# Packed attention and a gated feed-forward block on one core: the first entry's query softmax in four pieces of tokens, another form of the weight conversion, and a new order of all steps

## The chip, the cores and the metric

The program runs on one core of one Trainium2 chip. The metric is device microseconds of one execution, the median of several runs; lower is better. Five engines work beside each other, each on its own list of instructions: TensorE (PE in the profile), VectorE (DVE), ScalarE (ACT), GpSimd (POOL) and SyncE (SP), which issues nearly all transfers.

## The reference

```python
def _attn_ref(q, k, v, p):             # q, k, v: (8, 8, 576, 64); p: (8, 8, 32, 64)
    def sm_attn(qq, kk, vv):           # softmax over the last axis, scale 1/8
        ...
    p_packed = sm_attn(p, k, v)        # 32 packed rows read 576 tokens
    return sm_attn(q, p_packed, p_packed)

def _moe_ref(x, w_in, w_spatial, b_spatial, w_out):   # x: (8, 576, 512)
    h = np.maximum(x @ w_in, 0.0)                     # 512 -> 1024
    u, v = h[..., :512], h[..., 512:]
    v_n = (v - mean(v)) / sqrt(var(v) + 1e-6)         # over features
    v_s = einsum('ts,bsd->btd', w_spatial, v_n) + b_spatial
    return (u * v_s) @ w_out                          # 512 -> 512
```

`w_in` and `w_out` arrive as float64 and are turned into float32 on the chip. All the rest is float32.

## The kernel before, in words

The batch has eight entries. Each goes through the same stages, all on chip: packed scores, maximum, exponential and sum (`pack_*`), the packed rows (`packed*`), the query scores and their softmax over 32 packed rows (`query_*`), the feed-forward values (`value`, `relu`, `moments`, `mean`, `inverse`, `norm*`), the spatial gate (`gate*`) and the output product (`product`, `put`). The output of the query softmax is never multiplied out: `mix` multiplies the packed rows by `w_in`, so that `value` and `up` are products of the softmax weights `a` with those mixed weights `m`. Every float32 factor of a large product is split into a rounded high part and the rest (`*_hi` on ScalarE, `*_lo` on VectorE or GpSimd, by `rest`), and three products hi·hi, hi·lo, lo·hi are made. From entry 1 on, the gate and the output product are done with seven block products in place of eight; entry 0 does the gate plainly (`gate`, all of `hm`, `l` and `t` terms) because its spatial weights are still being prepared (`spatial_hi`, `spatial_rest`, `spatial_lo`; `spatial_rest(c)` is the identity pass `x - high(x)` on TensorE, four passes of 288 columns in float32 and two rounded ones).

There are four PSUM tiles of two banks, `ps0` to `ps3`; every product takes one with `on(i)` and must wait until its last reader, often a copy on ScalarE, is done. SBUF tiles have tags with one or two buffers; the mixed weights `m_h`, `m_l` have one buffer each, the query weights `a_h`, `a_l` too.

The order of work is written out by hand: `InOrder` with `PIN = "tvsg"` pins TensorE, VectorE, ScalarE and GpSimd to the order of the calls in the program's text. An instruction that waits holds up all that stand behind it on its engine. In the text below a call such as `F6.norm_lo(2)` is a step of the feed-forward of entry 6, `A7.mix(0)` one of the attention of entry 7; while entry b runs, the attention of entries b+1, b+2 and b+3 is being prepared.

Steps that the prediction speaks of: `to_f32`, the conversion of a float64 weight (a generator; each `next` issues its next part); `pack_max` and `pack_exp` (maximum and exponential of the packed scores); `pack_turned_part` (copies of the turned weights from PSUM into `p1T`); `query_spread`, `query_max`, `query_sub`, `query_exp`, `query_add`, `query_total`, `query_inverse`, `query_norm`, `query_turn`, `query_hi`, `query_lo` (the softmax over 32 rows, in this order, on tile `sm_t`, then `extra`, then `a_h`, `a_l`); `mix_hi`, `mix_lo`, `mix_keep` (PSUM to `m_h`, `m_l`, or to `kept` first); `packed_turned` (PSUM to `ppT`); `gate_add`, `gate_mult`, `block_lo` (tiles `o`, `u`, `g_l`). Nearly all instructions are recorded at line 43 of the kernel, the wrapper, so the rows go by tiles.

Of the kernel before, what the change touches and what calls it, by code (L numbers as in the profile page):

```python
# [49 lines left out]
def body(ctx: ExitStack, tc, q, k, v, vt, p, w_in, w_sp, b_sp, w_out, out):  # L50
# [311 lines left out]
    class Attention:  # L362
# [28 lines left out]
        def pack_most(self, r):  # L391
# [40 lines left out]
        def pack_turn(self, t1, t2):  # L432

            p1 = self.p1
            self.t1, self.t2 = t1(), t2
            for r in range(2):
                for c in range(NC):
                    x = r * TAIL + c * P  # L440
                    flip(self.t1[:, r, c * P : (c + 1) * P], p1[:, r, x : x + P])
            flip(self.t2[:, 1, :P], p1.rearrange("p r s -> p (r s)")[:, NC * P : NC * P + P])
# [16 lines left out]

        def pack_values(self, psum):  # L460
            v_sb = loaded.pop(("v", self.b))
            self.pv = psum()
# [1779 lines left out]
```

## Time and profile before

| | |
|---|---|
| median of 3 runs | 392.48 us (392.11 to 392.54) |
| span of the profiled execution | 391.2 us |
| median of the runs less that span | 1.3 us, what lies around it |
| busy share of the span: PE, DVE, ACT, POOL | 96%, 83%, 72%, 39% |
| the chain that ended last, shares | PE 77%, DVE 10%, ACT 6%, POOL 3%, DMA 2%, issue 1% |
| first large product (`value` of entry 0) | 27.41 us from the span's start |
| end of the last product | 387.16 us |

A busy PE here is the time from the start of a product to its modelled end, which for a 288-column product is some 0.3 us, while the next one starts some 0.13 us after it; so the share of 96% hides waits of up to 0.2 us before each product, and the starts of products tell more than the share. The profiled execution is not one of the three timed ones; its span is taken as the base of the sum and 1.3 us is put on top.

### The profile page before, as it was taken

The numbers are of one execution on the slowest core, as the hardware profiler recorded it, in microseconds if no ns is written. First come the engines' busy times: TensorE is split into PE (matmuls) and PEld (weight loads), VectorE is DVE, ScalarE is ACT, GpSimd is POOL, SyncE is SP. The second block draws the span as 40 slices with busy tenths as digits, with TensorE's granted clock in tenths as the row PEclk, the third lists the DMA queues.
The fourth block names the chain that finished last, engine by engine and source line by source line (L and its number), as shares of the span: only waits on it lengthen the run. The fifth ranks groups of instructions, "written<-read, shape, count | busy, mean of one in ns | idle before, by whom it ended". The sixth has DMA issues, their size and how long they took to land.

```text
span 391.2 us, 8947 instructions
## 1 busy us (share of the span) xinstructions
PE 376.8 (96%) x3674; PEld 337.8 (86%) x3674; DVE 326.5 (83%) x502; ACT 280.3 (72%) x494; POOL 153.5 (39%) x190
## 2 busy tenths in 40 slices
PE   6889999999999999999999999999899999999995
PEld 5668978799798898998899898998699889999995
DVE  2898989995799959997799959997599969997784
ACT  3588876978975598766985598666895589558642
POOL 3467647899461040702143040703153043504120
PEclk9899999999999999999999999999999999999999
DMA  7999149630510803045300803033000600002003
GB/s 302 416 391 368 68 137 361 252 111 12 185 69 0 335 29 131 0 164 201 116 10 0 331 34 124 0 122 121 4 1 2 241 3 2 0 34 89 2 0 122
DMA packets 17660, 47.79 MB, mean 122 GB/s; under 512 B 1362, under 2 KB 11602, under 8 KB 14804
## 3 DMA queue, kind: packets, MB, share of 16 engines
q1 hardware_dynamic: 17332, 47.02, 32.3%
q8 instruction: 29, 0.48, 0.5%
q10 hardware_dynamic: 288, 0.21, 0.2%
q14 instruction: 11, 0.09, 0.1%
HBM read 37.79 MB, written 9.44 MB: 121 GB/s over the span
## 4 chain that ended last, share of the span: by engine, by line
PE 77%; DVE 10%; ACT 6%; POOL 3%; DMA 2%; issue 1%; SPq 0%; DVEq 0%; ACTq 0%
PE ps_t L43 77%; DMA kT<-in_k 2%; DVE u L43 2%; DVE o L43 1%; ACT vr L43 1%; DVE bn L43 1%; POOL bits L43 1%; DVE vr L43 1%; DVE sm_t L43 1%; POOL sm_t L43 1%; POOL rstd L43 1%; DVE v_l L43 1%; DVE m_l L43 1%; DVE sm L43 1%; ACT sm_t L43 0%
## 5 line engine op out<-in xcount | busy, mean ns | idle before, releaser
L43 POOL TENSOR_TENSOR u<-o,u 128x576 f32<-128x576 f32 x14 | 24.1, 1722 | 71.1 <-DVE o L43 70.6
L43 PE MATMUL ps_t<-t,wout_h 128*128 128x288 f32 x232 | 50.2, 300 | 0.1
L43 POOL TENSOR_TENSOR rstd<-mv,eps 128x2 f32<-128x2 f32 (+2 forms) x26 | 5.8, 222 | 107.2 <-DVE mv L43 107.2
L43 PE MATMUL ps_t<-wb_h,v_h 128*128 128x288 f32 x144 | 40.7, 300 | 0.5 <-ACT kept L43 0.3
L43 PEld LDWEIGHTS ps_t<-t,wout_h 128*128 128x128 f32 x232 | 37.8, 188 | 3.0 <-DVE t L43 2.4
L43 PE MATMUL ps_t<-wb_l,v_h 128*128 128x288 f32 x144 | 39.9, 295 | 0.0
L43 PE MATMUL ps_t<-a_h,m_h 128*128 128x288 f32 x128 | 38.6, 301 | 1.1 <-ACT ppT L43 1.1
L43 DVE TENSOR_TENSOR v_l<-vr,v_h 128x512 fp32r<-128x512 f32 x45 | 31.7, 727 | 7.9 <-ACT v_h L43 7.9
L43 PE MATMUL ps_t<-a_l,m_h 128*128 128x288 f32 x128 | 37.8, 295 | 0.0
L43 PE MATMUL ps_t<-a_h,m_l 128*128 128x288 f32 x128 | 37.8, 295 | 0.0
L43 PE MATMUL ps_t<-t,wout_l 128*128 128x288 f32 x116 | 32.4, 295 | 0.0
L43 PEld LDWEIGHTS ps_t<-wb_h,v_h 128*128 128x128 f32 x144 | 27.0, 188 | 5.1 <-issue 1.4
L43 PE MATMUL ps_t<-g_h,wout_h 128*128 128x288 f32 x104 | 29.2, 296 | 0.9 <-ACT pp L43 0.9
L43 PE MATMUL ps_t<-wsums,v_h 128*128 128x288 f32 x168 | 29.3, 296 | 0.0
L43 PE MATMUL ps_t<-g_h,wout_l 128*128 128x288 f32 x104 | 29.1, 295 | 0.0
L43 ACT CAST v_h<-vr 128x512 fp32r<-128x512 f32 x46 | 27.3, 624 | 2.3 <-DVE vr L43 1.6
L43 PE MATMUL ps_t<-wb_h,v_l 128*128 128x288 f32 x144 | 28.5, 294 | 0.0
L43 PEld LDWEIGHTS ps_t<-wb_l,v_h 128*128 128x128 f32 x144 | 27.1, 188 | 0.0
L43 PE MATMUL ps_t<-m_h,a_h 128*128 128x512 f32 x80 | 26.0, 392 | 0.1
L43 PEld LDWEIGHTS ps_t<-a_h,m_h 128*128 128x128 f32 x128 | 24.0, 188 | 2.3 <-ACT ppT L43 1.3
L43 DVE BATCH_NORM_STATS2 bn<-vr 128x6 f32<-128x512 f32 x32 | 21.1, 681 | 5.7 <-ACT vr L43 5.7
L43 PE MATMUL ps_t<-m_l,a_h 128*128 128x512 f32 x80 | 25.9, 390 | 0.0
(178 smaller groups left out, 1188.4 us busy)
## 6 DMA issues: line engine op xcount, KB each, us to landing
v_sb<-in_v SPq DMA_DIRECT2D x8, 1024.0 KB, 6.6
kT<-in_k SPq DMA_DIRECT2D x7, 1152.0 KB, 5.1
qT<-in_q SPq DMA_DIRECT2D x7, 1152.0 KB, 5.1
out_t<-prod SPq DMA_DIRECT2D x27, 288.0 KB, 2.4
raw<-in_w_in SPq DMA_DIRECT2D x4, 1024.0 KB, 9.4
raw<-in_w_out SPq DMA_DIRECT2D x2, 1024.0 KB, 7.9
kT<-in_k SPq DMA_DIRECT2D x2, 576.0 KB, 7.1
qT<-in_q SPq DMA_DIRECT2D x2, 576.0 KB, 12.4
```

What stands on the lines that cost most here:

```text
L43: return lambda *a, **k: self.tc.keep_in_program_order(call(*a, **k))
```

## The change

What it does, in five parts:

1. `to_f32`: the test for tiny numbers stands first (`max` of the magnitude with a least value, in place) and the last pass that multiplied by the outcome of a comparison is gone; GpSimd's sum writes the result. For the two halves of `w_in` that are needed first, the magnitude is taken on VectorE and no longer on ScalarE.
2. `pack_max` of entry 0 takes the maximum by halves of the keys, the first while the second half is still to come; scale and the smaller of both (negated) maxima are one instruction. The turned weights are copied row by row, one row on VectorE.
3. The query softmax of entry 0 runs in four pieces of tokens (128, 160, 96 and 192 of 576) in place of two halves.
4. `spatial_rest` makes its identity passes two and two.
5. All steps from the first to the last entry stand in a new order; the PSUM tile that a product takes changes with it. Two warming products of 2 (`keep_warm`) are left out.

```diff
-        dve.tensor_scalar(
-            bits, high, 3, 0x3FFFFFFF, op0=ALU.logical_shift_left, op1=ALU.bitwise_and
-        )
...
+        if eng is act:
+            act.activation(size, high.bitcast(F32), AF.Abs)
+        else:
+            eng.tensor_scalar(bits, high, 0x7FFFFFFF, None, op0=ALU.bitwise_and)
+        yield
+        dve.tensor_scalar_max(size, size, LEAST)
+        yield
+        dve.tensor_scalar(
+            bits, bits, 3, 0x3FFFFFFF, op0=ALU.logical_shift_left, op1=ALU.bitwise_and
+        )
+        yield
         dve.scalar_tensor_tensor(
             bits, high, -0x40000000, bits, op0=ALU.bitwise_and, op1=ALU.bitwise_or
         )
         yield
         for j in range(raw.shape[1]):
-            pool.tensor_tensor(bits[:, j], bits[:, j], low[:, j], op=ALU.add)
-        yield
-        size = high.bitcast(F32)
-        act.activation(size, size, AF.Abs)
-        yield
-        dve.scalar_tensor_tensor(
-            dst, size, LEAST, bits.bitcast(F32), op0=ALU.is_ge, op1=ALU.mult
-        )
+            pool.tensor_tensor(dst[:, j].bitcast(I32), bits[:, j], low[:, j], op=ALU.add)
...
         for h in range(2):
-            hs = slice(h * HS, (h + 1) * HS)
-            mm(ps[:, h, :HS], ident, x[:, hs], True, False)
+            mm(ps[:, h, :HS], ident, x[:, h * HS : (h + 1) * HS], True, False)
+        for h in range(2):
             mm(ps[:, h, :HS], minus, rows_of(wb_h, wt_h, c)[:, h], False, True)
...
+            self.spans = [(0, 0, HS), (1, 0, HS)]
+            if self.by_half:
+                self.spans = [(0, 0, 128), (0, 128, HS), (1, 0, 96), (1, 96, HS)]
...
+        def pack_max_half(self, r, x):
+            if x == 0 and r == 0:
+                self.first = small.tile([P, 2], F32, tag="first", name="first")
+            to = (self.nmax if x else self.first)[:, r : r + 1]
+            dve.tensor_reduce(to, self.s1[r][:, x, :HS], axis=AX.X, op=ALU.max, negate=True)
+
+        def pack_scale_both(self, r):
+            nmax = self.nmax[:, r : r + 1]
+            dve.tensor_scalar(
+                nmax, nmax, self.first[:, r : r + 1], SCALE, op0=ALU.min, op1=ALU.mult
+            )
...
+        def pack_turned_row(self, r, eng=act):
...
+            copy(
+                self.p1T[:, :NC, r, :],
+                self.t1[:, r, :].rearrange("p (c x) -> p c x", c=NC),
+            )
```

Every `query_*` step now takes the number of a piece and works on that part of the tiles, as this one does:

```diff
-        def query_exp(self, i):
-            act.activation(self.t[i], self.t[i], AF.Exp, scale=SCALE)
+        def query_exp(self, k):
+            i, lo, hi, n = self.cut(k)
+            t = self.t[i][:, n, :]
+            act.activation(t, t, AF.Exp, scale=SCALE)
```

The order, at three places. First VectorE in entry 0, from the query scores on (`sm_t` is the softmax tile, `mx` and `sm` its maxima and sums, `extra` the turned weights). Before:

```order
L43 STREAM_TRANSPOSE sm_t<-ps_t 128x576
L43 TENSOR_REDUCE mx<-sm_t 128x18
L43 STREAM_TRANSPOSE sm_t<-ps_t 128x576
L43 TENSOR_REDUCE mx<-sm_t 128x18
L43 TENSOR_REDUCE sm<-sm_t 128x18
L43 TENSOR_SCALAR sm<-sm 128x18
L43 RECIPROCAL sm<-sm 128x18
L43 TENSOR_REDUCE sm<-sm_t 128x18
L43 TENSOR_SCALAR sm<-sm 128x18
L43 RECIPROCAL sm<-sm 128x18
L43 STREAM_TRANSPOSE extra<-sm_t 128x576
L43 TENSOR_TENSOR m_l<-ps_t,m_h 128x1024
```

And with the change, the same stretch from its second half on:

```order
L43 TENSOR_TENSOR sm_t<-sm_t,sm 128x256
L43 RECIPROCAL sm<-sm 128x10
L43 TENSOR_REDUCE mx<-sm_t 128x12
L43 STREAM_TRANSPOSE extra<-sm_t 128x256
L43 TENSOR_REDUCE sm<-sm_t 128x6
L43 STREAM_TRANSPOSE extra<-sm_t 128x320
L43 TENSOR_SCALAR sm<-sm 128x6
L43 TENSOR_TENSOR m_l<-ps_t,m_h 128x1024
L43 RECIPROCAL sm<-sm 128x6
L43 TENSOR_REDUCE sm<-sm_t 128x12
L43 TENSOR_SCALAR sm<-sm 128x12
L43 RECIPROCAL sm<-sm 128x12
```

The first turned piece (256 columns, 128 tokens) now comes out while the last two pieces are still being summed, and `m_l`, the rest of the mixed weights, stands behind the second turned piece.

Second, ScalarE at the end of entry 0, ahead of its first output product (`t`, `g_h` and `wout_h` are high parts of that product's factors, `m_h` that of entry 1's mixed weights, `pp` the packed rows of entry 2, whose PSUM tile the product takes). Before:

```order
L43 CAST t<-u 128x576
L43 CAST m_h<-ps_t 128x1024
L43 CAST g_h<-u 128x576
L43 CAST a_898<-bits 128x512
L43 ACTIVATE sm_t<-sm_t 128x576
L43 CAST g_h<-u 128x576
L43 ACTIVATE sm_t<-sm_t 128x576
L43 ACTIVATE pp<-ps_t,rtot 128x64 x2
```

With the change:

```order
L43 CAST t<-u 128x576
L43 CAST wout_h<-bits 128x512
L43 ACTIVATE sm_t<-sm_t 128x576
L43 CAST g_h<-u 128x576
L43 ACTIVATE rtot<-tot,tiny 128x2
L43 ACTIVATE sm_t<-sm_t 128x576
L43 ACTIVATE sm<-sm,tiny 128x18 x2
L43 CAST g_h<-u 128x576
L43 ACTIVATE pp<-ps_t,rtot 128x64 x2
L43 CAST g_h<-u 128x576
L43 CAST wout_h<-bits 128x512
L43 CAST m_h<-ps_t 128x1024
```

`m_h` stood ahead of all of them and now stands behind `pp`.

Third, ScalarE in entry 5 (`ppT` is the copy by `packed_turned`, `p1T` that by `pack_turned_part`, `vr` the values and their normalisation, `u` the output of `up`). Before, with the program's buffer numbers:

```order
L43 ACTIVATE vr_3552<-ps3_t_3514 128x1024
L43 COPY p1T_3572<-ps2_t_3538 128x2x4x128
L43 ACTIVATE vr_3510<-vr_3510,off_3576,rstd_3512 128x512 x2
L43 COPY p1T_3572<-ps1_t_3499 128x128
L43 CAST v_h_3489<-vr_3510 128x512
L43 ACTIVATE vr_tail_3527<-vr_tail_3527,off_3601,rstd_3529 64x512
L43 ACTIVATE vr_3552<-vr_3552,off_3611,rstd_3554 128x512 x2
L43 ACTIVATE u_3642<-ps0_t_3559 128x576
L43 COPY ppT_3645<-ps1_t_3499 128x128
```

With the change:

```order
L43 ACTIVATE vr_tail_3544<-vr_tail_3544 64x512
L43 COPY ppT_3573<-ps1_t_3520 128x128
L43 ACTIVATE vr_3575<-ps3_t_3531 128x1024
L43 ACTIVATE rtot_3194<-tot_3193,tiny_78 128x2
L43 COPY p1T_3599<-ps2_t_3559 128x2x4x128
L43 ACTIVATE vr_3523<-vr_3523,off_3593,rstd_3525 128x512 x2
L43 COPY p1T_3599<-ps1_t_3520 128x128
L43 ACTIVATE u_3628<-ps0_t_3580 128x576
```

`ppT` stood last of nine and now comes second; the last reader of PSUM tile `ps1` is now the small `p1T` copy.

## Rows read from the trace of the kernel before

**Rows 1.** The page, part 1: busy time, share of the span and instructions of each engine.
```profile
PE 376.8 (96%) x3674; PEld 337.8 (86%) x3674; DVE 326.5 (83%) x502; ACT 280.3 (72%) x494; POOL 153.5 (39%) x190
```

**Rows 2.** Busy time of the engines in three stretches (start:end, length, then each engine's busy us and instructions, granted clock, DMA share, GB/s): the time ahead of the first value product, ten microseconds inside entry 3, and the stretch of entry 0's output products.
```profile
0.00:27.41 27.41, 21.06 (x241) 15.53 (x241) 17.18 (x27) 15.38 (x24) 13.20 (x21) 0.94 0.94 366
200.00:210.00 10.00, 10.00 (x77) 10.00 (x76) 9.18 (x14) 7.08 (x15) 7.96 (x5) 1.00 0.01 2
70.00:100.00 30.00, 29.12 (x268) 26.53 (x264) 22.84 (x32) 24.66 (x50) 28.44 (x29) 1.00 0.34 122
```

**Rows 3.** Who PE waited for between 27 and 388 us: us in total, times, the longest.
```profile
PE ps_t L43 <- DVE g_l L43: 1.4, 3, 0.6
PE ps_t L43 <- ACT ppT L43: 1.1, 1, 1.1
PE ps_t L43 <- ACT pp L43: 0.9, 1, 0.9
PE ps_t L43 <- ACT kept L43: 0.3, 1, 0.3
```

**Rows 4.** The timeline of the first 17 us: start, length, engine, what. The conversion of `w_in`, the packed softmax and the packed rows of entry 0.
```profile
6.10 0.69 DVE L43 TENSOR_SCALAR bits<-raw 128x1024 int32<-128x1024 int32 x1 [4.54 <-DMA raw<-in_w_in]
6.82 1.23 DVE L43 SCALAR_TENSOR_TENSOR bits<-raw,bits 128x1024 int32<-128x1024 int32 x1
...
8.29 2.54 POOL L43 TENSOR_TENSOR bits<-bits,raw 128x512 int32<-128x512 int32 x2 [5.51 <-DVE bits L43]
...
10.56 0.76 DVE L43 TENSOR_REDUCE nmax<-ps_t 128x1 f32<-128x576 f32 x1 [2.51 <-PE ps_t L43]
...
11.61 0.74 ACT L43 ACTIVATE p<-ps_t,nmax 128x576 f32<-128x576 f32 x1 [2.37 <-DVE nmax L43]
...
14.24 1.17 ACT L43 COPY p1T<-ps_t 128x128 f32<-128x128 f32 x2
14.44 3.33 POOL L43 TENSOR_TENSOR bits<-bits,raw 128x512 int32<-128x512 int32 x2 [3.61 <-ACT raw L43]
15.28 1.29 DVE L43 TENSOR_SCALAR rtot<-tot 128x2 f32<-128x2 f32 x1
...
16.95 0.29 DVE L43 TENSOR_TENSOR pp<-ps_t,rtot 128x128 f32<-128x128 f32 x1 [0.18 <-PE ps_t L43]
```

**Rows 5.** The same timeline from 17 to 28 us: entry 0's query scores and softmax, two halves of an identity pass, the first value product.
```profile
17.81 1.23 DVE L43 SCALAR_TENSOR_TENSOR w_in_sb<-raw,bits 128x1024 f32<-128x1024 f32 x1 [0.57 <-POOL bits L43]
17.98 1.20 PE L43 MATMUL ps_t<-qT,ppT 64*32 64x288 f32 x32 [0.36 <-ACT ppT L43]
...
18.95 0.78 DVE L43 STREAM_TRANSPOSE sm_t<-ps_t 128x576 f32<-128x576 f32 x1
...
20.59 1.16 POOL L43 TENSOR_TENSOR sm_t<-sm_t,mx 128x576 f32<-128x576 f32 x1 [2.82 <-DVE mx L43]
...
25.41 0.65 PE L43 MATMUL ps_t<-st_tail,ident 128*128 128x288 f32 x2
...
25.95 1.19 DVE L43 TENSOR_TENSOR m_l<-ps_t,m_h 128x1024 fp32r<-128x1024 f32 x1
26.03 0.65 PE L43 MATMUL ps_t<-st_tail,ident 128*128 128x288 f32 x2
26.09 0.67 ACT L43 CAST a_h<-extra 128x576 fp32r<-128x576 f32 x1
...
27.41 0.70 PE L43 MATMUL ps_t<-m_h,a_h 128*128 128x512 f32 x2
```

**Rows 6.** The timeline of PE at entry 0's first gate products, and where they go on after a wait.
```profile
36.41 0.40 PE L43 MATMUL ps_t<-wb_h,v_h 128*128 128x288 f32 x1
...
37.66 0.40 PE L43 MATMUL ps_t<-wb_h,v_h 128*128 128x288 f32 x1 [0.19 <-ACT v_h L43]
```

**Rows 7.** The timeline of ACT and PE between 47 and 49 us, at the end of entry 0's gate.
```profile
47.26 1.18 ACT L43 COPY u<-ps_t 128x576 f32<-128x576 f32 x2 [0.35 <-PE ps_t L43]
47.59 1.22 PE L43 MATMUL ps_t<-wb_h,v_l 128*128 128x288 f32 x8
```

**Rows 8.** The timeline of ACT and PE between 68 and 73 us, ahead of entry 0's first output product.
```profile
68.32 1.02 ACT L43 CAST m_h<-ps_t 128x1024 fp32r<-128x1024 f32 x1 [2.06 <-PE ps_t L43]
...
70.64 1.09 PE L43 MATMUL ps_t<-w_in_sb,ppT 64*32 64x512 f32 x16
72.61 0.40 PE L43 MATMUL ps_t<-g_h,wout_h 128*128 128x288 f32 x1 [0.88 <-ACT pp L43]
```

**Rows 9.** The timeline of ACT at 103 us and of DVE at 118 to 121 us, in entry 1.
```profile
103.25 1.02 ACT L43 COPY kept<-ps_t 128x1024 f32<-128x1024 f32 x1
...
117.94 2.02 DVE L43 TENSOR_TENSOR u<-o,u 128x576 f32<-128x576 f32 x1
119.89 0.74 DVE L43 TENSOR_REDUCE sm<-sm_t 128x18 f32<-128x576 f32 x1
```

**Rows 10.** The timeline of ACT between 270 and 277 us, in entry 5.
```profile
270.20 1.03 ACT L43 ACTIVATE vr<-ps_t 128x1024 f32<-128x1024 f32 x1 [0.17 <-PE ps_t L43]
...
273.44 0.26 ACT L43 COPY p1T<-ps_t 128x128 f32<-128x128 f32 x1
...
276.77 0.26 ACT L43 COPY ppT<-ps_t 128x128 f32<-128x128 f32 x1
```

**Rows 11.** The timeline of DVE at 320 us, in entry 6.
```profile
320.01 0.68 DVE L43 TENSOR_TENSOR v_tail<-vr_tail,v_tail 64x512 fp32r<-64x512 f32 x1
```

More of the change, by code (lines that the diff above doesn't have):

```diff
@@ new lines, in body @@
+    F2.up_relu(0)
+    F2.up(2, psum=on(0))
+    F2.v_hi("A11")
+    F2.offset(1)
+    F2.tail_hi()
+    F2.norm_act(1)
+    F2.v_lo("A11")
+    A4.pack_values(on(2))
+    F2.up_relu(2)
+    F2.v_sum("S1")
+    A3.query_scores(psum=by_turns(1, 0))
+    F2.up_relu(3)
+    load_v(5)
+    F2.v_sum("S2")
+    A4.packed(act)
+    A3.mix(1, psum=on(3))
+    F2.v_hi("S2")
+    A3.query_spread(0)
+    F2.v_hi("S3")
+    A3.query_spread(1)
+    A3.mix(0, psum=on(2))
+    F2.v_hi("A12")
+    F2.v_lo("S2")
@@ new lines, in body @@
+    F2.product(A22, "T4", onto=S3)
+    A3.query_total(1, act)
+    A5.pack_total(act)
+    A3.query_inverse(1)
+    F2.keep_part("U", S2)
+    F2.block_lo("T1")
+    F2.keep_part("P3", S4)
+    A3.query_norm(1)
+    F2.product(S1, "T1", onto=S2)
+    A3.query_hi(0)
+    A3.query_turn(1)
+    A3.query_lo(0)
+    A3.query_hi(1)
+    F3.value(0, psum=on(3), rs=(0,))
+    F2.add_part("P1", A12)
+    A3.query_tail(0, act)
+    A3.query_lo(1)
+    F2.put(F2.part("P1"), 0, 0)
+    F3.value(0, rs=(1,))
@@ new lines, in body @@
+    A4.query_norm(0)
+    F3.keep_part("P7", S3)
+    F3.block_hi("T1")
+    F3.block_lo("T4")
+    F3.product(A22, "T4", onto=S3)
+    F3.keep_part("U", S2)
+    A4.query_turn(0)
+    A6.pack_total(act)
+    F3.keep_part("P3", S4)
+    F3.block_lo("T1")
+    A4.query_hi(0)
+    F3.product(S1, "T1", onto=S2)
+    A4.query_turn(1)
+    A4.query_lo(0)
+    A4.query_hi(1)
+    F3.add_part("U", A22)
+    F4.value(0, psum=on(1), rs=(0,))
+    F3.add_part("P1", A12)
+    F3.put(F3.part("U"), 1, 0)
+    A4.query_lo(1)
@@ new lines, in body @@
+    F4.moments(1, 0)
+    F4.up(3, psum=on(0))
+    F4.v_hi("A11")
+    F4.mean(1, 0)
+    F4.mean(1, 1)
+    F4.up_relu(2)
+    F4.v_lo("A11")
+    F4.inverse(1)
+    F4.v_hi("S3")
+    F4.norm_lo(2)
+    A5.query_scores(psum=by_turns(2, 3))
+    F4.up_relu(3)
+    F4.offset(1)
+    F4.v_lo("S3")
+    F4.norm_act(1)
+    A6.pack_values(on(1))
+    A5.query_spread(0)
+    A5.query_spread(1)
+    A5.mix(1, psum=on(0))
+    A6.packed(act)
+    load_v(7)
+    F4.v_sum("S1")
+    A5.mix(0, psum=on(1))
@@ new lines, in body @@
+    A5.query_norm(0)
+    F4.block_hi("T4")
+    F4.keep_part("P3", S4)
+    F4.block_lo("T4")
+    F4.product(A22, "T4", onto=S3)
+    F4.block_lo("T1")
+    F4.keep_part("U", S2)
+    A5.query_turn(0)
+    A5.query_norm(1)
+    F4.product(S1, "T1", onto=S2)
+    A5.query_hi(0)
+    A5.query_turn(1)
+    A5.query_lo(0)
+    A5.query_hi(1)
+    F5.value(0, psum=on(0), rs=(0,))
+    F4.add_part("P1", A12)
+    A5.query_tail(0, act)
+    A5.query_lo(1)
+    F4.put(F4.part("P1"), 0, 0)
+    F5.value(0, rs=(1,))
@@ new lines, in body @@
+    F7.moments(1, 1)
+    F6.put(F6.part("P3"), 0, 1)
+    F7.up(1, psum=on(2))
+    F7.offset(0)
+    F7.moments(1, 0)
+    F7.norm_hi(2)
+    F7.norm_act(0)
+    F7.mean(1, 1)
+    F7.mean(1, 0)
+    F7.tail_hi()
+    F7.norm_lo(2)
+    F7.up(2, psum=on(0))
+    F7.inverse(1)
+    F7.up_relu(0)
+    F7.v_sum("S3")
+    F7.offset(1)
+    F7.v_hi("A11")
+    F7.up(3, psum=on(1))
+    F7.norm_act(1)
+    F7.v_lo("A11")
+    F7.gate_product(1, psum=on(3))
+    F7.v_sum("S1")
+    F7.v_hi("A12")
+    F7.up_relu(1)
```

2511 lines of the change are left out of this document (1379 added, 1132 removed).

## The prediction

> **What bounds the kernel now.** I read the busy shares first, then stretches, then who TensorE waits for, then the timeline at each place where it waits. PE is busy for 96% of the span [rows 1]. In the middle of the run it is full: ten microseconds of entry 3 hold 77 products of 288 columns, one every 0.13 us, at the full granted clock (1.00, which is 2.4 GHz) [rows 2]. A new order cannot make that stretch shorter, since the change leaves the number of large products as it is. So the change can win in two places only: ahead of the first value product at 27.41 us, where PE's work is short and other engines set the pace, and at PE's remaining waits. From 27 us on these come to 3.7 us by the list of waits: 1.4 for `g_l`, 1.1 for `ppT`, 0.9 for `pp`, 0.3 for `kept` [rows 3]. By the starts of products each is 0.1 to 0.2 longer, since a modelled end hides part of it, and I take them so: 1.2 for `ppT`, 1.0 for `pp`, 0.5 for `kept`, and 0.6, 0.8 and 0.4 for the three of `g_l`. What a win ahead of 27 us is worth is read further down, where PE first runs without a wait; what a win at a later wait is worth is the wait itself, because PE goes on without slack behind it.
>
> **The head, step by step.** *Conversion.* The first half took one pass and a two-tensor pass, 0.72 and 1.23 us from start to start [rows 4]. It now takes three passes of 0.72 (the magnitude on VectorE too) and the long one: 6.10 + 3 x 0.72 + 1.23 = 9.49 us. The packed scores are ready at 10.56 only [rows 4], so this costs nothing.
>
> *Packed maximum.* One reduction of 576 columns takes 0.76 [rows 4]. One of 288 must lie between half of it, 0.38, and all of it; I take 0.46, near the lower end, since such passes go by columns. The first exponential then starts at 10.56 + 0.46 + some 0.2 for the scale = 11.25 in place of 11.61 [rows 4]: 0.36 earlier.
>
> *Turned weights.* Both copies stood on ACT from 14.24 for 1.17 us, behind a conversion pass [rows 4]. With one row on VectorE the packed values are done about a microsecond earlier. But `pp` stands on VectorE behind the second half's conversion, which starts after the maxima, near 11.9: three passes of 0.72, the copy (0.6, half of 1.17), 0.4 of small ones and of waiting for the turns, and 1.23 end near 16.3, and `pp` began at 16.95 [rows 4]. So 0.6 is won, and the query scores start near 17.4 in place of 17.98 [rows 5].
>
> *Query softmax.* VectorE's last conversion pass (17.81, 1.23 long) held the first transpose back to 18.95 [rows 5]; it is gone, worth 0.8. From there the first piece alone has to pass through. With 0.15 us fixed and 1.05 ns a column (0.78 for 576 [rows 5]) its passes are 0.42 each; GpSimd's at 2.0 ns a column (1.16 for 576 [rows 5]). Adding up VectorE's list down to the first turned piece gives 24.5, its cast on ACT 24.9, the first value product near 25.0: 2.4 us before 27.41. This is not what PE wins. One identity pass less is done by then, two halves of 0.62 (25.41 to 26.03 [rows 5]) or 1.24 us, and it comes back among the value products. And PE now waits between pieces: `m_l` (1.19) begins near 25.3, hardly before its 25.95 [rows 5], so the products with `m_l` start near 26.5, and I add up 0.7 of waiting. 2.4 - 1.24 - 0.7 = 0.5. By the first gate product ScalarE and VectorE have caught up, so that the wait ahead of 37.66 (0.35 by starts, [rows 6]) need not be there: **head, -0.8**, with -1.3 and +0.2 as its ends. Two and two identity passes hold as many columns: nothing. The two missing warming products stood in idle time: nothing.
>
> **The waits behind it.** *Ahead of entry 0's first output product*, PE is late by 1.0 (0.88 by the row at 72.61 [rows 8]). The ACT row shows why: `m_h` has one buffer, and its cast waited 2.06 us at the head of ACT's list for the last product that read it [rows 8], with `pp` six instructions behind. In the new list `m_h` stands behind `pp`: -1.0. *Entry 1 at 103 us*: the gate product needs the tile that the 1.02 us copy to `kept` frees [rows 9]; the query scores, 1.2 us of products [rows 5], now lie between them: -0.5. *Entry 1 at 121 us*: `g_l` was late by 0.6 behind a sum of 0.74 [rows 9], which now stands further ahead: -0.6. *Entry 5*: `up` waited 1.2 for `ppT`, last on ACT at 276.77 [rows 3, 10]. Now the tile's last reader is the small `p1T` copy, at 273.44 before, 3.2 us after the values' end at 270.2 [rows 10]. With `ppT` and a small sum ahead of it that is 3.7 us, and PE has turns and two `up` products, 1.2 + 2 x 12 x 0.13 = 4.4 us, to do first: -1.2, with 0.7 to spare. *Entry 6*: `g_l` was late by 0.8 at the end of a VectorE stretch without gaps from 319 us; the 0.68 us `norm_lo(2)` [rows 11] moves out of it to where VectorE waits: -0.7. *Entry 7*'s wait of 0.4 keeps its chain: nothing.
>
> **What the new order adds.** In entry 0's gate, four products (0.53 us) now lie between the copy that frees the next packed scores' tile and these, where eight did, and the two copies take 1.18 [rows 7]: +0.3. `spatial_lo(2)` stands behind two conversion passes on ACT: +0.3. The query scores of entry 1 wait for an exponential: +0.2. `mix(0)` of entry 1 needs the tile that `m_l` frees, whose `m_h` is now late: +0.5. Entries 2 to 4, which have no wait to lose, are in a new order too: I take +0.3, of 0 to 1.0.
>
> **Sum.** -0.8 - 1.0 - 0.5 - 0.6 - 1.2 - 0.7 = -4.8; +1.3 and +0.3; together **-3.2 us**. On the span of 391.2 that is 388.0, and with the 1.3 that the median of 392.48 lies above that span, 389.2. The ends: all wins at their best (-5.6, head -1.3 among them) and nothing added gives 386.9; the head's bad end, half of the later wins and twice the added waits gives about 392.
>
> **Rivals.**
>
> *The head is held by GpSimd.* The tiny pass on `rtot`, 128x2, took 1.29 us, and ended where GpSimd's first conversion sum of 14.44 ended [rows 4]; the second passes of the softmax sums behave so too. The new scale of the packed maximum comes at 11.05, just when GpSimd's second sum of the first half starts (9.7 + 1.27, half of 2.54 [rows 4]). If it has to wait, it waits until 12.25, and 1.0 of the head is lost again: **390.2**. For it: the `rtot` row. Against: `rtot` has two columns, this has one, and it may slip in between the two sums. The Trainium skill ("SBUF — State Buffer", section "Who interferes with whom") says that such a VectorE pass and a GpSimd instruction exclude each other for a whole instruction and that the later one blocks; the `rtot` row agrees with that.
>
> *The waits only move.* Every list is new, and a wait removed at one place comes back at the next one. For it: VectorE is busy 83%, and in entry 0's output stretch GpSimd 28.4 of 30 us [rows 1, 2], so late work has no room to catch up. Against: each wait above has a cause of its own that the new lists take away. Time: 392.5, within 0.8.
>
> *GpSimd becomes the bound in entry 0* (the one on the slower side). Between 56 and 76 us it has some thirteen long instructions in a row: conversion sums, the rests of `wout` and `g`, parts of the softmax. The second output product (A12 with g21) needs two of these, and I find only 0.7 us of slack. Its conversion sums are 1.27 alone and took 3.33 for two beside VectorE [rows 4], 0.4 more each. Thirteen times 0.4 is 5.2; from 0.7 late on PE waits one for one, +4.5, against the -3.2: **393.8**. It is slower than before once GpSimd is late by some 4 us. Against: it was as full before (28.4 of 30 us [rows 2]) and PE did not wait there.
>
> **How the numbers follow.** Forecast, around 389.2 (386.9 to 390): 0.50. Held head, around 390.2: 0.20. A smaller win, 391 to 391.6: 0.06. Waits only move: 0.10. GpSimd: 0.14. A measurement can tell 0.2%, 0.8 us, from no change; so faster 0.76, same 0.10, slower 0.14. 386.9 to 392.1 leaves out GpSimd's case, part of the moved waits and a little below: 2 in 10.
>
> **What would show it.** In the profile after: the first value product near 25 us and the first gate product near 35.7; no wait of PE for `pp`, `ppT` or `kept`; `g_l` under 0.6 in all; entries 2 to 4 at 43.9 us each as now. Wrong would be: a first gate product after 36.8, a wait of PE for `wout_l` or `g_l` by GpSimd in the first output products, or new waits in entries 2 to 4 that add up to more than 1 us.

## The result and the profile after

| kernel | runs | median, us | lowest to highest | ratio to before (95%) |
|---|---|---|---|---|
| before | 4 | 392.45 | 392.11 to 392.54 | |
| changed | 4 | 396.24 | 395.25 to 399.0 | 1.0101 (1.0072 to 1.013) |

The changed kernel is **slower by 1.0%**. The medians are 3.79 us apart. Its profiled execution is its quickest run: 395.25 us, span 393.5, 2.3 over the span of before; so what follows shows 2.3 us of the loss, and why the other three runs are 0.6 to 3.8 us longer is only in part known (below, clock and maxima). One execution of `e1_warm`, the profiled one, ran at half speed throughout (736.98 us): its trace is not used, and the median given for it is that of its other five. Page, part 1, as [rows 1]:
```profile
PE 377.7 (96%) x3666; PEld 333.8 (85%) x3666; DVE 326.3 (83%) x522; ACT 277.3 (70%) x496; POOL 158.1 (40%) x193
```
Nothing there tells where 2.3 us went; shorter stretches tell more. Busy time up to the first value product, from there to the first gate product, and over entry 0's output products (columns as in [rows 2]):
```profile
0.00:25.13 25.13, 18.52 (x227) 13.06 (x228) 15.56 (x39) 9.81 (x19) 9.98 (x19) 0.93 0.94 361
25.13:36.87 11.74, 10.90 (x49) 8.06 (x47) 10.49 (x23) 10.50 (x20) 8.89 (x14) 1.00 1.01 415
...
70.00:100.00 30.00, 30.00 (x313) 26.48 (x306) 20.04 (x33) 22.73 (x46) 27.24 (x26) 1.00 0.34 122
```
Who PE waited for between 27 and 388 us (the first lines), as [rows 3]:
```profile
PE ps_t L43 <- ACT p1T L43: 1.1, 2, 0.8
PE ps_t L43 <- ACT u L43: 0.8, 2, 0.5
PE ps_t L43 <- DVE v_tail L43: 0.8, 1, 0.8
PE ps_t L43 <- DVE vr_tail L43: 0.7, 1, 0.7
PE ps_t L43 <- ACT pp L43: 0.5, 1, 0.5
PE ps_t L43 <- DVE g_l L43: 0.3, 1, 0.3
PE ps_t L43 <- DVE v_l L43: 0.3, 1, 0.3
...
```
The waits of [rows 3] are gone, smaller, or at another place (`pp`); new ones took their place. The table goes by PE's starts in the two timelines (us). An entry is taken from its first value product to that of the next entry; the forecast column adds up the prediction's own terms:

| stretch | before | changed | forecast | measured |
|---|---|---|---|---|
| start to entry 0's first gate product | 36.41 | 36.87 | -0.8 | +0.46 |
| on to entry 1's first value product | 49.32 | 49.75 | +0.1 | +0.43 |
| entry 1, to entry 2's first value | 46.17 | 45.06 | -0.9 | -1.11 |
| entries 2 to 4, likewise | 131.69 | 133.43 | +0.3 | +1.74 |
| entry 5 | 44.26 | 44.36 | -1.2 | +0.10 |
| entry 6 | 41.23 | 41.50 | -0.7 | +0.27 |
| entry 7, to the end of the last product | 38.07 | 38.41 | 0 | +0.34 |
| sum | 387.15 | 389.38 | -3.2 | +2.23 |

So one term came as said, entry 1. Here are four places where the others failed, read in the timeline of the changed kernel (cut at the dots). First, the packed maximum (compare [rows 4]):
```profile
9.86 2.53 POOL L43 TENSOR_TENSOR w_in_sb<-bits,raw 128x512 int32<-128x512 int32 x2 [7.94 <-DVE bits L43]
...
10.60 0.82 DVE L43 TENSOR_REDUCE first<-ps_t 128x1 f32<-128x288 f32 x2 [0.98 <-PE ps_t L43]
11.34 0.45 DVE L43 TENSOR_REDUCE nmax<-ps_t 128x1 f32<-128x288 f32 x1
11.82 0.21 DVE L43 TENSOR_SCALAR nmax<-nmax,first 128x1 f32<-128x1 f32 x1
...
12.14 0.74 ACT L43 ACTIVATE p<-ps_t,nmax 128x576 f32<-128x576 f32 x1 [4.78 <-DVE nmax L43]
```
A half takes 0.45 us, as estimated. But none starts before the last scores are there, and three of them stand ahead of the first exponential: it starts at 12.14 in place of 11.61. Second, ahead of the first gate product:
```profile
35.37 0.58 ACT L43 COPY part<-ps_t 64x512 f32<-64x512 f32 x1
35.38 0.83 DVE L43 TENSOR_TENSOR v_l<-vr,v_h 128x512 fp32r<-128x512 f32 x1 [0.44 <-ACT v_h L43]
...
36.13 0.68 DVE L43 TENSOR_TENSOR vr_tail<-ps_t,part 64x512 f32<-64x512 f32 x1
...
36.87 0.40 PE L43 MATMUL ps_t<-wb_h,v_h 128*128 128x288 f32 x1 [0.66 <-DVE vr_tail L43]
```
PE needs the tile that the add for the tail (`vr_tail`, the last 64 rows) frees. The add stands behind `v_l` on DVE, and its operand `part` behind two splits on ACT. Third, entry 4:
```profile
233.80 0.66 POOL L43 TENSOR_TENSOR rstd<-mv,eps 128x2 f32<-128x2 f32 x1 [2.61 <-DVE mv L43]
...
234.54 1.12 POOL L43 TENSOR_TENSOR rstd<-rstd,neg_half 128x2 f32<-128x2 f32 x1
...
236.26 1.52 ACT L43 ACTIVATE vr<-vr,off,rstd 128x512 f32<-128x512 f32 x2 [0.97 <-POOL off L43]
...
237.68 0.49 ACT L43 ACTIVATE pp<-ps_t,rtot 128x64 f32<-128x64 f32 x2
```
`norm_act(1)` stands at the head of ACT's list 0.97 us for GpSimd's offset, and the packed copy, for which PE waits 0.5, is behind it. Fourth, entry 5 (compare [rows 10]):
```profile
272.76 0.27 ACT L43 COPY ppT<-ps_t 128x128 f32<-128x128 f32 x1 [1.65 <-PE ps_t L43]
272.92 1.03 ACT L43 ACTIVATE vr<-ps_t 128x1024 f32<-128x1024 f32 x1
...
274.03 1.01 ACT L43 COPY p1T<-ps_t 128x1024 f32<-128x1024 f32 x1
...
275.09 0.40 PE L43 MATMUL ps_t<-a_h,m_h 128*128 128x288 f32 x1 [0.78 <-ACT p1T L43]
```
The copy that was moved to the front waits 1.65 us for PE's turns (transposes), and `relu(1)` and the large `p1T`, which PE needs, stand behind it.

### The profile page after: what moved, and what is told of

It reads as the page before. It is cut to its first block, busy times and chain, and to the rows that moved or that the text cites. A ratio compares the mean times of both kernels' runs of the same rounds, so it can differ in the third digit from the quotient of the medians.

```text
span 393.5 us, 8964 instructions
## 1 busy us (share of the span) xinstructions
PE 377.7 (96%) x3666; PEld 333.8 (85%) x3666; DVE 326.3 (83%) x522; ACT 277.3 (70%) x496; POOL 158.1 (40%) x193
## 4 chain that ended last, share of the span: by engine, by line
PE 68%; DVE 11%; ACT 9%; DMA 4%; POOL 3%; issue 2%; SPq 1%; DVEq 0%; POOLq 0%; ACTq 0%
PE ps_t L43 68%; ACT vr L43 3%; DVE bits L43 2%; DMA kT<-in_k 2%; DMA again<-in_w_sp 2%; DVE bn L43 2%; POOL rstd L43 2%; DVE sm_t L43 1%; DVE vr_tail L43 1%; POOL again L43 1%; DVE u L43 1%; ACT p1T L43 1%; ACT v_tail L43 1%; ACT v_h L43 1%; DVE m_l L43 1%
## 5 line engine op out<-in xcount | busy, mean ns | idle before, releaser
L43 POOL TENSOR_TENSOR rstd<-mv,eps 128x2 f32<-128x2 f32 (+2 forms) x26 | 10.0, 385 | 117.5 <-DVE mv L43 114.0
L43 DVE TENSOR_TENSOR v_l<-vr,v_h 128x512 fp32r<-128x512 f32 x45 | 35.4, 800 | 7.1 <-ACT v_h L43 6.9
L43 POOL TENSOR_TENSOR u<-o,u 128x576 f32<-128x576 f32 x14 | 25.1, 1791 | 30.2 <-DVE o L43 29.6
L43 POOL TENSOR_TENSOR sm_t<-sm_t,mx 128x576 f32<-128x576 f32 (+3 forms) x16 | 23.8, 1493 | 17.2 <-DVE mx L43 17.0
```

The costliest lines, as they stand in the source:

```text
L43: return lambda *a, **k: self.tc.keep_in_program_order(call(*a, **k))
```

## Experiments

Times are medians; "first value" and the like are PE's starts in the profiled execution of that run. The kernel before was timed beside each run (392.7 to 393.2 us, by the chip); ratios are to that time.

**Halves of the program.** Run `e2_head_new`: entry 0 changed, the rest as before. Run `e3_rest_new`: the reverse.
From `e2_head_new`, cut:
```diff
     sp_sum(T2, pool)
+    out_hi(S3)
...
+    b = 1
+    att, nxt, far = nxt, far, further
...
-    out_hi(S3)
-    F1.value(0, psum=on(0), rs=(0,))
...
```


> Entry 0 as in the changed kernel up to entry 1's first value product, then the body of the kernel before for entries 1 to 7. Theory A (each stretch loses by its own list): the changed kernel reached that point 0.89 us later than the kernel before, so 392.5 + 0.9 = 393.4 us. Rival (what entry 0 leaves undone at its end, or the clock that it leaves, costs the entries behind it): 395 us or more. If entries 1 to 7 give back what is late at their start: 392.5.

Measured 395.95. The profiled execution had its first value at 27.77, 2.64 later than the changed kernel (a low clock up to 19 us: below), entry 1's at +4.05 and its end at +4.66 us against before. From entry 2's first value on the old lists keep the distance within 0.1 (255.34 us where before has 255.24), so the loss lies ahead of that. First gate to entry 1's first value takes 50.29 (before 49.32) and entry 1 46.69 (before 46.17): entry 0 and the seam behind it lose. The 393.4 was too low; the time is the rival's, but not by entries 2 to 7. With the head's 0.46 the three stretches make 1.95 us of the 3.3 measured; the rest is open.

> Entry 0 as in the kernel before, then the changed kernel's list for entries 1 to 7. Theory A: the changed kernel lost 2.23 - 0.89 = 1.34 us after entry 1's first value product, so 392.5 + 1.3 = 393.8 us. Rival (the loss of entries 2 to 7 follows from entry 0, by the clock or by work left over): 391.5 to 392.5, since entry 1's list won 1.1 us by itself.

Measured 395.68. Entry 1's first value is at 85.57 (before 85.73), then entries 2 to 7 take 258.31 us, 3.07 over before (257.70 in the changed kernel, 2.46 over). Theory A's sign holds, its size does not: the new lists of entries 2 to 7 lose 2.5 to 3 us behind either entry 0. Entry 1 wins nothing (46.12) behind the old entry 0: PE has a new wait there, 1.07 us for `p1T` at 97.55.

**One move alone, in the kernel before.** Run `e4_mix` (three steps, as the change puts them):
```diff
-    nxt.mix_hi(1)
     ff.gated(2, True)
...
-    nxt.mix_lo(1)
     far.pack_values(on(3))
...
-    nxt.mix(0, on(0))
     far.packed(act)
+    nxt.mix_hi(1)
+    nxt.mix_lo(1)
...
     ff.product(A11, "g11", psum=on(3), to="o11")
+    nxt.mix(0, on(0))
```


> The kernel before with one of the change's moves alone: the split of entry 1's mixed keys (m_h, m_l of part 1) goes behind the packed copy of entry 2 on ACT and DVE, and part 0's product behind the first output product, so that the packed copy no longer stands behind a copy that waits 2.06 us for TensorE. By the prediction's term for it: the wait of 1.2 us at 71 goes, 1.0 us less, 391.5 us. Rival (the wait moves to the next link, the gated product's split or entry 1's first value): 392.2 to 392.5 us.

Measured 394.53, ratio 1.0044 (1.003 to 1.0058). PE's waits between 60 and 100 us:
```profile
PE ps_t L43 <- ACT pp L43: 0.7, 1, 0.7
PE ps_t L43 <- ACT p L43: 0.7, 1, 0.7
PE ps_t L43 <- DVE m_l L43: 0.3, 1, 0.3
```
The wait moved, as the rival has it, and the time is worse than the rival's: one wait of 0.88 [rows 8] became three, 1.7 in sum. `pp` itself keeps 0.7 of it here.

Run `e10_before5`:
```diff
     far.pack_turned_part(1)
+    nxt.packed_turned(act)
     ff.v_sum("S3")
...
-    nxt.packed_turned(act)
     ff.norm_hi(2)
```


> The kernel before with one move: entry 5's copy of the turned packed values goes from the end of ACT's list for that stretch to right behind the second copy of the turned probabilities. By the prediction's term for entry 5 the wait of 1.26 us at 277 us goes and 1.0 to 1.2 us are won: 391.5 to 391.7 us beside the kernel before's 392.5 to 392.7. Rival (the bank's next owner finds another wait at once, as in the move at 71 us): no gain beyond 0.3 us.

Measured 391.86, ratio 0.9974 (0.9959 to 0.999); entry 5 takes 42.93 us instead of 44.26, 1.33 less. The term of 1.2 was there to be won; the change put the copy in the wrong place.

**The places in the changed kernel.** Run `e5_f5`:
```diff
-    A6.packed_turned(act)
     F5.relu(1)
...
     A7.pack_turned_part(0)
+    A6.packed_turned(act)
```


> The changed kernel with one step of entry 5 put back: on ACT the copy of the turned packed values (ppT of entry 6) goes behind entry 5's relu(1) and the first copy of the turned probabilities (p1T of entry 7), instead of ahead of both, where it waited 1.65 us for TensorE's nine turns. Theory A (that copy at the head of ACT's list is why entry 5 did not win its 1.2 us): TensorE's gap of 0.94 us at 274 us goes and entry 6's first value comes 0.7 to 0.9 us earlier against entry 5's (43.5 to 43.7 us between them instead of 44.36). Rival (the turned copies wait for the same turns in any order, the rank only renames the wait): 44.2 to 44.5 us between them.

Measured 394.81. On ACT (all starts are late by the head's 3.7 us, see below):
```profile
275.86 1.02 ACT L43 ACTIVATE vr<-ps_t 128x1024 f32<-128x1024 f32 x1 [0.61 <-PE ps_t L43]
...
276.97 1.00 ACT L43 COPY p1T<-ps_t 128x1024 f32<-128x1024 f32 x1
277.86 0.27 ACT L43 COPY ppT<-ps_t 128x128 f32<-128x128 f32 x1
```
Entry 5 takes 43.29 us instead of 44.36: theory A, 1.07.

Run `e6_mid`:
```diff
+    F2.up_relu(2)
     F2.norm_act(1)
...
-    F2.up_relu(2)
...
     F4.mean(0, 1)
+    F4.moments(1, 0)
...
     F4.norm_act(2)
+    F4.mean(1, 0)
+    F4.mean(1, 1)
...
-    F4.moments(1, 0)
...
-    F4.mean(1, 0)
-    F4.mean(1, 1)
```


> The changed kernel with the order of the kernel before at two places in front of norm_act(1): in entry 2 the rectified copy up_relu(2), whose bank the query scores need, goes ahead of norm_act(1) on ACT; in entry 4 the second moments of block 1 and their means go back ahead of the first gates' work on DVE, so that GpSimd's offsets come before ACT reaches norm_act(1). Theory A (norm_act(1) waiting for GpSimd's offset at the head of ACT's list holds the packed copy and a rectified copy, on which TensorE waits): TensorE's gaps of 0.69 us at 147 and 1.07 us at 238 us go; the three entries 2 to 4 take 1.0 to 1.4 us less (132.0 to 132.4 us from entry 2's first value to entry 5's instead of 133.43). Rival (those entries are held by something else, and the waits come back at the next bank): 133.2 us or more.

Measured 395.55. Entry 4: 43.90 us instead of 44.65, and no wait for `pp`: shown. Entry 2: 45.18 instead of 44.60: the reading failed there. `up_relu(2)` waits for PE itself, and put first it holds up `norm_act(1)` (the pass over `vr`) and the next copy:
```profile
146.56 0.65 ACT L43 ACTIVATE u<-ps_t 128x576 f32<-128x576 f32 x1 [0.89 <-PE ps_t L43]
147.10 1.51 ACT L43 ACTIVATE vr<-vr,off,rstd 128x512 f32<-128x512 f32 x2
```

Run `e7_pool`:
```diff
     F0.norm_hi(1, (0,))
+    F0.norm_lo(1, (0,), pool)
...
-    F0.norm_lo(1, (0,), pool)
     F0.norm(2)
```


> The changed kernel with GpSimd's remainder of entry 0's gate values (v_l of block 1, first half) ahead of the second weight conversion's sums, where the kernel before had it, instead of between two of them. Theory A (VectorE's pass over vr_tail took 2.77 us instead of 0.53 because GpSimd's two-input passes held the memory port that they share): the pass takes 1.3 us or less, the wait of 0.80 us for v_tail at 48.8 us goes, and entry 0's first output product comes 0.6 to 1.0 us earlier against its first gate (34.5 to 34.9 us between them instead of 35.54). Rival (the pass is stretched by the second sum as well, which stays): the pass stays over 2 us and nothing moves.

Measured 395.35. The pass over `vr_tail`, in the changed kernel and here:
```profile
44.60 2.77 DVE L43 TENSOR_SCALAR vr_tail<-vr_tail,mv,rstd 64x512 f32<-64x512 f32 x1 [0.44 <-POOL rstd L43]
45.47 1.54 DVE L43 TENSOR_SCALAR vr_tail<-vr_tail,mv,rstd 64x512 f32<-64x512 f32 x1 [0.44 <-POOL rstd L43]
```
The wait for `v_tail` went with it. But between first gate and first output product lie 35.28 us instead of 35.54, where 34.5 to 34.9 were expected, since the same GpSimd pass now met another pass of DVE:
```profile
40.23 2.21 POOL L43 TENSOR_TENSOR v_l<-vr,v_h 128x512 fp32r<-128x512 f32 x1 [0.89 <-ACT v_h L43]
...
41.21 1.52 DVE L43 TENSOR_SCALAR vr<-vr,mv,rstd 128x512 f32<-128x512 f32 x1
...
43.48 0.40 PE L43 MATMUL ps_t<-wb_h,v_h 128*128 128x288 f32 x1 [0.62 <-ACT v_h L43]
```
Cause shown, gain mostly moved.

Run `e8_tail`:
```diff
+    F0.relu(2)
     F0.norm_hi(0, (1,))
...
-    F0.relu(2)
+    F0.relu_tail()
     F0.norm_lo(0, (0,), dve)
...
-    F0.relu_tail()
```


> The changed kernel with the tail block of entry 0 ahead in two lists: ACT copies its half (part) before the splits of block 0, and VectorE adds it before the remainder of block 0. Theory A (the first gate waited 0.66 us for the bank that only the tail's add sets free, so the list decided it, after TensorE had been busy from 26 to 36 us): the first gate comes 0.5 to 0.8 us earlier, at 36.1 to 36.4 us instead of 36.87. Rival (the splits that were put back are what the gate then waits for): 36.7 us or later, with a wait for v_h or v_l.

Measured 395.73. The first value came 0.56 sooner here, the first gate 1.23 (35.64), so 0.67 by the edit: theory A for the wait. The first output product is only 0.37 sooner: the rest is given back inside the gate, where PE now waits for a copy that stands behind two conversion passes on ACT:
```profile
38.82 0.40 PE L43 MATMUL ps_t<-wb_h,v_h 128*128 128x288 f32 x1 [0.81 <-ACT wb_l L43]
```

Run `e9_sum`: the edits of `e5_f5`, `e7_pool` and entry 4's of `e6_mid`, and
```diff
-    F2.up(3, psum=on(3))
+    F2.up(2, psum=on(0))
...
-    F2.up(2, psum=on(0))
+    F2.up(3, psum=on(3))
```


> The changed kernel with the places put back that the four runs before showed to cost, and entry 2's third and fourth key products in the old order (part 2 before part 3, so that the bank which the query scores need is written 1.6 us sooner): entry 5's copy (1.07 us), entry 4's moments (0.75 us), entry 0's remainder on GpSimd (0.3 to 0.7 us), entry 2's order (0.5 to 0.7 us). Theory A (each wait is its own and the sums add): 2.4 to 3.2 us less than the changed kernel, a span of 390.3 to 391.1 us where TensorE's clock is at 0.996, and entry 2 takes 43.9 to 44.1 us again. Rival (the waits share their causes): a span over 391.8 us.

Measured 396.39, the rival's side. Entries 4 and 5 keep their gains (43.81, 43.30), entry 2 takes 46.54, 1.94 more: part 2's tile is freed by a copy that the new list has late.
```profile
144.49 0.25 ACT L43 COPY p1T<-ps_t 128x128 f32<-128x128 f32 x1
...
144.79 0.40 PE L43 MATMUL ps_t<-a_h,m_h 128*128 128x288 f32 x1 [1.41 <-ACT p1T L43]
```
My second cause for entry 2 fell too. Of what was tried, only the old list as a whole (43.8 to 43.9 in the runs that have it) removes the loss.

**Clock and maxima.** Run `e1_warm`:
```diff
     A0.pack_values_tail()
+    keep_warm(2, 2)
...
     A0.query_lo(0, pool)
+    keep_warm(3, 2)
```


> The changed kernel with the four warming products put back that its list had dropped (two ahead of the copy of the packed values, two ahead of entry 0's first value product); nothing else differs. Theory A (the time is lost in waits of the new lists, and the granted clock of TensorE only spreads its runs): no gain, 395.3 to 396.7 us, mean clocks between 0.98 and 0.996 as in the changed kernel's runs. Theory B (the missing products let the clock fall, and that is part of the loss): 395.0 us or less in the median with the clock at 0.996 in every run, 1.2 us under the changed kernel's median of 396.24.

Measured 395.92 (395.23 to 398.03), much the same spread: theory B falls. But in its runs and the changed kernel's, nine in all, the time follows the mean granted clock: 395.23 at 0.999, 395.25 at 0.996, 396.65 at 0.990, 398.03 at 0.985, 399.0 at 0.979. Elsewhere it follows less well: `e2_head_new` took 395.92 at 0.999 and 395.11 at 0.996. The trace of `e5_f5` shows where the clock is low:
```profile
6.00:8.00 2.00, 0.01 (x2) 0.04 (x4) 1.80 (x3) 1.15 (x1) 0.00 (x0) 1.00 1.00 401
8.00:10.00 2.00, 1.35 (x32) 0.40 (x32) 1.51 (x2) 0.00 (x0) 0.21 (x1) 0.66 1.02 420
...
20.00:24.00 4.00, 3.20 (x41) 1.30 (x49) 1.70 (x5) 0.27 (x1) 1.16 (x2) 0.50 1.05 359
```
PE stands idle from 6 to 8 us; its clock falls to 0.50 (1.2 GHz) and stays there until some 25.7; its first value is at 28.85, 3.7 late. In the profile of the changed kernel the same fall lasted until 11.7, in `e2_head_new` until 19.1.

Run `e11_both`: entries 0 and 1 of `e7_pool`, entries 2 to 7 of `e10_before5`. Run `e12_both_warm`: the same with
```diff
-    keep_warm(1, 11)
+    keep_warm(1, 17)
```


> The changed kernel's entries 0 and 1 (GpSimd's remainder put back as tried before), then the body of the kernel before for entries 2 to 7 with entry 5's copy moved. Theory A (stretches add): entry 2's first value comes at 131.1 us as in the run with that remainder, 0.8 us sooner than before, and entries 2 to 7 keep their 255.2 us less 1.0 in entry 5: a span of 389.3 to 389.6 us at a clock of 0.996, and 390.8 to 391.6 us in the median of timed runs, under the kernel before. Rival (the new head's dependence on TensorE's clock in its first 25 us eats it): 392 us or more in the median.

> The same as the run beside it, with 17 instead of 11 warming products at the start, so that TensorE runs through to the first packed scores at 8.0 us instead of standing idle from 5.8 us. Theory C (the fall of the granted clock to a half at 8 to 9 us follows from that idle stretch, and the new head pays for its length): the clock stays at 1.00 from 8 to 24 us in the profile and 0.999 or more in every run, the spread of the runs shrinks under 1 us, and the median is 0.3 to 0.8 us under the run beside it. Rival (the fall does not hang on the idle stretch): the same clocks and times as beside it, or 0.2 us more where the warming products delay the first scores.

Measured 392.16 (ratio 0.9988, 0.997 to 1.0007) and **390.74** (0.9965, 0.9947 to 0.9982). Stretches add behind entry 1: entries 2 to 7 of `e11_both` take 253.95, 1.3 under before. But its time is the rival's, level with before: its first value is at 26.47, with the clock low up to 15 us. In the trace of `e12_both_warm`:
```profile
6.00:8.00 2.00, 1.79 (x23) 1.61 (x29) 1.69 (x3) 1.19 (x1) 0.00 (x0) 1.00 1.01 408
8.00:10.00 2.00, 1.36 (x33) 0.38 (x18) 1.71 (x3) 0.00 (x0) 0.10 (x1) 1.00 1.03 423
```
No fall; the last packed scores take 0.72 us instead of 1.22, and the first value is at 25.03 instead of 26.47. Ten of twelve runs show 0.999 or more, two 0.991. Theory C holds for the trace; the gain, 1.42, is larger than it said (0.3 to 0.8), and the spread shrank only from 4.0 to 2.8 us, where it said under 1.

Runs `e13_warm` and `e14_before5_warm` have the same line in the changed kernel and in `e10_before5`.

> The changed kernel with 17 instead of 11 warming products at the start and nothing else. Theory C (the stretch at half clock behind the idle of 5.8 to 8 us explains the spread of the changed kernel's runs, and 0.5 to 0.8 us of its loss in the median): clock 0.999 or 1.0 in most runs, first gate at 36.2 to 36.4 us, a span of 392.8 to 393.1 us and a median of 394.5 to 394.9 us: still 2 us over the kernel before, which is the lists' part. Rival (most of the loss is the clock): 393 us or less in the median.

Measured 396.0, runs within 0.25 us, where 394.5 to 394.9 was expected. The loss is not the clock. That the spread is, these four runs do not show: the four of `e15_warm_whole` (below), with the same line, reach from 395.0 to 397.53 at clocks of 0.995 to 1.0. The first output product came 0.54 sooner, entry 2's first value 0.93 later. At entry 1's output products, `e13_warm`:
```profile
119.39 1.43 POOL L43 TENSOR_TENSOR u<-o,u 128x576 f32<-128x576 f32 x1
119.51 1.93 DVE L43 TENSOR_TENSOR u<-o,u 128x576 f32<-128x576 f32 x1
```
and in the changed kernel:
```profile
119.25 2.03 POOL L43 TENSOR_TENSOR u<-o,u 128x576 f32<-128x576 f32 x1
119.27 0.70 DVE L43 TENSOR_TENSOR u<-o,u 128x576 f32<-128x576 f32 x1
```
Of two passes that meet, one is longer by much of the other: VectorE, which PE follows, pays 1.2 us in the first run, GpSimd 0.6 in the second. Before, VectorE paid [rows 9], and there, too, it started only 0.02 after GpSimd:
```profile
117.92 1.43 POOL L43 TENSOR_TENSOR u<-o,u 128x576 f32<-128x576 f32 x1
```
So the starts in a profile do not tell who will pay; what decides is open.

> The kernel before with entry 5's copy moved, as in the run at 391.86 us, and 17 warming products at the start. If the old head does not wait for TensorE (the slope of its runs against the clock was a third of the changed kernel's): 391.4 to 391.9 us, no more than 0.4 us won. Rival (any head gains as the new one does, 0.7 us on the scores): 391.0 to 391.3 us, level with the version of both kernels with 17 products (390.74).

Measured 391.11 (0.9958, 0.9943 to 0.9973), 0.75 under `e10_before5`, on another chip and with intervals that overlap. In the two profiles the first gate comes 0.57 sooner (35.91 beside 36.48). Both point to the rival: the old head gains too.

Runs `e15_warm_whole` and `e16_all`: in `e13_warm` and in `e12_both_warm`
```diff
-    A0.pack_max_half(0, 0)
...
-    A0.pack_max_half(1, 0)
-    A0.pack_max_half(0, 1)
+    A0.pack_most(0)
...
-    A0.pack_scale_both(0)
-    A0.pack_max_half(1, 1)
+    A0.pack_scale(0)
+    A0.pack_most(1)
...
-    A0.pack_scale_both(1)
+    A0.pack_scale(1)
```


> The changed kernel with 17 warming products and with whole packed maxima, as the kernel before had them, in place of four half maxima joined with the scale. Theory D (the halves cost: a half takes 0.45 us where a whole takes 0.76, and the first can start no sooner than the whole): the first exponential starts 0.3 to 0.5 us sooner than in the run beside it, and the first value comes 0.2 to 0.4 us sooner. Rival (the first value hangs on the query's softmax and the split of the mixed keys on VectorE, not on the maxima): the exponential is sooner, the first value stays within 0.15 us.

> The version of both kernels (entries 0 and 1 as changed, 2 to 7 as before with entry 5's copy moved, 17 warming products), with whole packed maxima. By theory D 0.2 to 0.4 us under the same without them: 390.3 to 390.6 us, 0.5% under the kernel before. Rival: 390.7 us, no difference.

The first exponential starts at 11.18 instead of 11.57; the first value did not move in `e15_warm_whole` (24.65 beside 24.64: the rival), the first gate came 0.30 sooner; `e16_all` has its first value 0.49 and its first gate 0.42 sooner, and its end 0.69. Times: 395.89 beside 396.0; **390.83** (0.9948, 0.993 to 0.9966) beside 390.74 on another chip: no difference that the times show; a cost of 0.3 to 0.4 us for the halves by the traces, one execution each. `e16_all` and `e12_both_warm` beat both kernels; so does `e14_before5_warm`, two lines away from the kernel before and within their intervals.

## Why the prediction was wrong

**Head: the step that failed is "By the first gate product ScalarE and VectorE have caught up".** They had not: PE waits 0.66 us ahead of that product for the tail's add, which stands behind `v_l` on VectorE and, by its operand, behind two splits on ScalarE; `e8_tail`, with the tail put ahead, had the gate 0.67 sooner. The wait ahead of 37.66 did nearly go (a gap of 0.14 is left), but it lies behind the first gate product. The first value came at 25.13, forecast 25.0, and the identity pass that comes back cost its 1.24. Then 2.28 won, less 1.24, less 0.34 for `m_l`, less 0.66 for the tail's add, less a remainder of some 0.5 that I have not traced, is 0.46 lost. I had added up DVE's list to the first value, not to the first gate. The halves of the maximum, counted as 0.36 won, lost 0.5 at the exponential: I let the first half start at 10.56 and forgot the two others ahead of the scale. That the first value came near its forecast all the same is luck in part; whether it hangs on the exponential at all is open (`e15_warm_whole` says no, `e16_all` yes).

**Entry 0 behind its gate** came near its terms in sum: +0.43 for +0.1. The wait for `pp` at 72.6 went, but `e4_mix` shows that this move alone costs; a wait's length is no price for removing it.

**Entry 1** came as said, in part by luck. The wait for `kept` went in every run with this list that has a trace. That for `g_l` went not only because the sum of [rows 9] stands further ahead, but because VectorE's pass did not wait for GpSimd's; in `e13_warm`, with the same list, it did, and entry 1 took 46.06 us instead of 45.06.

**Entries 2 to 4: the step that failed is "+0.3, of 0 to 1.0".** They stood near PE's bound, as the prediction says itself, so a new order had nothing to win there, and I priced what I had not read. 0.75 is entry 4's moments (shown), about 0.6 to 0.7 is entry 2's list (shown as a whole, its link open), 0.25 entry 3's (not tried).

**Entry 5: the step that failed is "the tile's last reader is the small `p1T` copy".** I followed that tile's readers and not what the moved copy holds up: at the head of ACT's list it waited 1.65, with the large `p1T` behind it, and PE waited 0.78 for that. Undone (`e5_f5`), 1.07 came back; well placed in the kernel before (`e10_before5`), 1.33 is won.

**Entries 6 and 7.** The wait for `g_l` in entry 6 went; its gate started 0.34 later from the entry's first value, and entry 7 lost 0.34. The cause was not tried and stays open.

**Rivals.** The held head: false, the 0.21 us scale ran beside GpSimd's second sum. Whether its single column is the reason, the prediction's own point against, no run tells. GpSimd as the bound: false, PE is busy for 30.00 of 30 us there. "The waits only move" named the mechanism, and its time, 392.5, was too kind: here they came back larger. No case that the prediction priced reaches 396.24. Of its signs of being wrong two came: the first gate after 36.8, and entries 2 to 4 longer by 1.74. All the gains were read where a wait ended and none from what stands behind the moved step, so the sum was one-sided.

**The ends of the range** do not follow from their own words. All wins at their best are -5.3 with a head of -1.3, not -5.6. The bad end (+0.2, half of the later wins, -2.0, and twice the added waits, +2.6 to +3.2) is 393.3 to 393.9, not about 392; the measured time lies above that, too.

**What stays open.** The medians differ by 3.79 us, the profiled runs by 2.3. The low clock in the head goes with the longer runs of the changed kernel, but `e13_warm`, without it in its trace, still takes 396.0. Its profiled execution lost elsewhere: entry 2's first value came 0.93 us later than in the changed kernel's.

## What to carry to other kernels

In hand-ordered lists a wait is worth its length only if the instruction put forward is ready when its turn comes and nothing behind it is on the path: check the list behind the moved step as well as the tile that it frees. Leave stretches that already run at the bound in their order. Try moves one at a time: the one place well chosen (`e10_before5`) won 0.26%. Six more warming products gave 0.2 to 0.4% by the medians in two kernels (`e12_both_warm`, `e14_before5_warm`), and nothing that the times show in the changed kernel (`e13_warm`).

## What the runs showed of the hardware

- In ten profiles with 11 warming products the clock fell to 0.50 behind PE's idle of about 2 us. The low stretch lasted from 3 to 17 us in the same head, by the run (8.3 to 11.7 in the changed kernel, 8.7 to 25.7 in `e5_f5`). In all five profiles with 17 it did not fall, and the packed scores took 0.72 us.
- A granted clock of 1.00 in the rows does not prove full speed early on. The warming products start 0.21 us apart at first and 0.11 once the clock is up, at 4.5 to 7.5 us, while the rows read 1.00 all the time before. In `e6_mid` and `e8_tail` the 0.21 lasts to their end, and the packed scores then took 1.21 us with 1.00 in the rows: there the clock had not fallen but not yet risen. All 22 warming records, in the changed kernel and in `e8_tail`, and the last scores in `e8_tail` and in `e12_both_warm`:
```profile
1.40 4.35 PE L43 MATMUL ps_t<-ident 128*128 128x128 f32 x22 [1.40 <-POOL ident masks.py:199]
1.39 5.06 PE L43 MATMUL ps_t<-ident 128*128 128x128 f32 x22 [1.39 <-POOL ident masks.py:199]
8.80 1.21 PE L43 MATMUL ps_t<-kT,pT 64*32 64x288 f32 x16 [0.15 <-DMA kT<-in_k]
9.15 0.72 PE L43 MATMUL ps_t<-kT,pT 64*32 64x288 f32 x16 [0.64 <-DMA kT<-in_k]
```
  The mean granted clock of these two runs is 0.999 and 1.0, so a mean near 1 does not rule out a slow head either.
- GpSimd and VectorE: of two passes that meet, one takes 0.6 to 1.3 us longer than alone (VectorE 1.93 and 2.02 against 0.70, GpSimd 2.03 against 1.43). The Trainium skill ("SBUF — State Buffer", section "Who interferes with whom") says of VectorE passes with two SBUF inputs that they contend with a GpSimd instruction that reads SBUF, and that issue order decides who blocks. These rows agree with the first; the second they do not show: with GpSimd's start 0.02 us ahead in both, VectorE paid before and GpSimd in the changed kernel.
